# Products with v of two head pairs at once, FFN columns on both sides of the turning, and a later place for VectorE's first weight conversion of a slot

## The chip, the cores and the metric

The kernel runs on one core of a Trainium2 chip. The metric is the device time of one execution in microseconds (us); runs are compared by their medians. Beside the times there is a profile of one execution, which lists every instruction of the engines: PE (TensorE), DVE (VectorE), ACT (ScalarE), POOL (GpSimd), and SP, which here issues nearly all DMAs.

## The reference

Threshold attention, followed by a bilinear feed-forward layer (FFN). All data are float32: 8 batches, 8 heads, 576 positions, head width 64; the FFN has 4608 tokens, width 512, inner width 1536.

```python
scores = (q @ k.T) / sqrt(64)                       # per batch and head: 576 x 576
scores = where(scores >= max(scores) - tau, scores, -1e9)
attn = exp(scores - max(scores)); attn = attn / (sum(attn) + 1e-9)
x = (attn @ v)                                      # heads side by side: 4608 x 512
out = ((x @ w_a) * (x @ w_b)) @ w_out
```

## The kernel before

**Units and slots.** Two heads of a batch form a pair (batch b, hp 0 to 3; 32 pairs). The 576 query rows of a pair are cut into four units of 128 rows (u = 0 to 3), and the last 64 rows of two neighbouring pairs form one more unit (u = 4). The list `units` holds all 144 of them; for the first batch it starts with u = 0 of the pairs 0 to 3, then u = 1 of the pairs 0 to 3, so units 0 and 1 belong to pairs 0 and 1, units 2 and 3 to pairs 2 and 3, and so on. The main loop (from L1117, `for g in range(...)`) makes one slot per unit, and later stages of earlier units are done in the same slot. The instructions of an engine run in the order in which this loop emits them: `keep_order` fixes it. So an instruction that waits holds up all that stand behind it on its engine.

**One slot.** `scores` (L404) multiplies q and k of unit g on PE into two PSUM tiles, `sc`. DVE takes the maximum of each row (L411) and the threshold (L412). `weigh` (L422 to L438) makes exponentials on ACT (L431, L432) and multiplies them by the threshold's mask on DVE (L435), which also gives the row sums. These masks are the last readers of `sc`. A reciprocal of the sums on DVE (L448) and a scaling on ACT (L454) normalise the weights. Then the weights have to be turned, since the product with v contracts over the keys.

**Two ways to turn.** The first eight units (`BY_PE = 8`) are turned on PE in the next slot, `turn_pe` (from L472): 18 matmuls (each shows as two in the profile, as all float32 matmuls do) against a diagonal matrix that holds the reciprocals; ACT copies eight of the nine turned blocks from PSUM (L485), DVE the ninth (L486). All later units are turned by DVE transposes of 32x32 blocks (`turn_blocks`, L502) and two DMAs through a scratch tensor (`swap`), which SP issues.

**Products with v.** For a unit that PE turned, `weighted_unit` (L594) runs two slots after its scores: `product` (L538 to L547) makes 36 matmuls of 64x64 with 64 moving columns, ACT copies one half of the result to x (L553) and DVE the other (L554, two copies of 64x64), and POOL copies x to a second tile `xS` with the halves of the partitions exchanged (L569). For the later units, `weighted` and `weighted_tails` do the same with more columns; `weighted_tails` (L619) already treats two pairs in one product (L629).

**FFN columns.** As soon as x of a block is there, the generator `ffn` emits its matmuls in steps. `advance(cols)` takes as many steps as make up `cols` moving columns, so FFN work fills PE between the attention's parts. In slots 0 to 8 this is one call a slot, behind the turning (L1204); later slots have four calls with fixed portions. The first block is made in pieces of 128 columns: products `pab` with w_a (copied by ACT, L860) and w_b (multiplied by DVE, L862).

**Weights.** The weights w_a, w_b and w_out are read as 36 pieces of 128x512 values in 64 bits and are brought to float32 bit by bit on the chip: `convert_first` on ACT (L298, L299), `convert_clamp` on POOL (L305), `convert_sign` (L311) and `convert_shift` (L319) on DVE, `convert_add` on POOL (L324). Slots 0 to 3 begin two pieces each, slots 4 to 9 three, slots 10 to 14 two. A piece that is begun in one slot gets its last three steps in the next, by `convert_rest(g, k)`: k = 0 for the slot's first piece, ahead of the masks (L1147), k = 1 and k = 2 for the others, behind the masks (L1202, L1205).

**PSUM.** All PSUM tiles come from one pool of four buffers (`banks`), each two banks long. A new tile takes a buffer whose readers are done, so a matmul can wait for a mask, a copy or an `h` product on DVE.

Of the kernel before, what the change touches and what calls it, by code (L numbers as in the profile page):

```python
# [23 lines left out]
BY_PE = 8  # L24
# [30 lines left out]
def kernel(  # L55
# [38 lines left out]
    nc = tc.nc  # L94
    B, H, S, D = q.shape
    P = 128
# [3 lines left out]
    HP = H // 2  # L100
    NT = 4
    MAIN = NT * P
    TAIL = S - MAIN
# [8 lines left out]
    NSLOT = 9  # L112
# [15 lines left out]
    def banks(n, name):  # L128

        return psum.tile([P, 2, 512], FP32, tag="banks", name=name)[:, :, 0:n]  # L130
# [4 lines left out]
    loaded = {}  # L135
# [90 lines left out]
    for f in range(NG):  # L226
        for c in range(HP):
            for dst, w in ((wa_sb, w_a), (wb_sb, w_b)):
                src = []
                for r in range(2):  # L230
                    chunks = [(2 * c + e) % HP * 2 + (r + (c >= HP // 2)) % 2 for e in range(2)]
                    cols = slice(f * CW + r * CH, f * CW + (r + 1) * CH)
                    rows = w[:, cols].bitcast(U32).rearrange("(k p) f -> p k f", p=D)
                    src.append(rows[:, chunks[0]:chunks[1] + 1:2])
                pieces.append((dst[:, f, 2 * c:2 * c + 2].rearrange("p k f -> p (k f)"), src))
    for F in range(NF):
# [3 lines left out]
    state = {"loaded": 0, "added": 0, "converted": 0, "rows": 0, "sums": False, "through": 0, "over": False,  # L240
             "layer": False, "paced": False, "all": False, "turn": 0, "due": NPIECES, "wide": True, "slot": 0, "reading": False, "first": 0}
# [114 lines left out]
    x_of, xtail_of = {}, {}  # L356
# [4 lines left out]
    def prep(i, name):  # L361

        flush((name, i))
        mT = loaded[i].pop(name).rearrange("p n e -> p (n e)")
        nc.vector.transpose(mT, mT)
        prepared.setdefault(i, {})[name] = mT
# [105 lines left out]
    def turn_pe(i, u):  # L472

        ws, dg = weights.pop((i, u))
        ws = [w.rearrange("p n e -> p (n e)") for w in ws]
        wT = turned_tile()[:, 0:G].rearrange("p g s e -> p (g s e)").rearrange("p (s w) -> p s w", w=P)
        turned[i, u, "pe"] = [wT[:, :, y * D:(y + 1) * D] for y in range(2)]
        tp = banks(512, "tp").rearrange("p y (s q) -> p y s q", s=NT)
        last = banks(P, "tp")
        for s in range(NSLOT):  # L480
            for j, w in enumerate(ws):
                to = (last[:, 0] if s == 2 * NT else tp[:, s // NT, s % NT])[j * D:(j + 1) * D]
                nc.tensor.matmul(to, w[:, s * D:(s + 1) * D], dg[:, j], start=True, stop=True)
        for y in range(2):
            nc.scalar.copy(wT[:, y * NT:(y + 1) * NT], tp[:, y])  # L485
        nc.vector.tensor_copy(wT[:, 2 * NT], last[:, 0])  # L486
# [51 lines left out]
    def product(wT, vm, n):  # L538

        pv = banks(n // 2, "pv")  # L540
        for s in range(NSLOT):
            for j in range(2):
                rows = slice(j * D, (j + 1) * D)
                for c in range(2):
                    y = j ^ c
                    nc.tensor.matmul(pv[c * D:(c + 1) * D, y], vm[rows, s], wT[y](rows, s),  # L546
                                     start=(s == 0), stop=(s == NSLOT - 1))  # L547
        return pv

    def settle(out, pv, c0, c1, others):  # L550

        n = c1 - c0
        one = [nc.scalar.copy(out[:, 0:n], pv[:, 0, c0:c1])]  # L553
        two = [nc.vector.tensor_copy(out[c * D:(c + 1) * D, n:2 * n], pv[(1 - c) * D:(2 - c) * D, 1, c0:c1])  # L554
               for c in range(2)]
        for mine, theirs in ((one, others[1] + two), (two, others[0] + one)):
            for a in mine:
                for b in theirs:
                    tc.declare_no_dep(a.ins, b.ins, reason="banks of their own")
        others[0].extend(one)  # L560
        others[1].extend(two)
# [4 lines left out]
    def exchange(x, xs, hp, c0, c1, engine):  # L566

        for r in range(2):
            engine.tensor_copy(xs[r * D:(r + 1) * D, hp, c0:c1], x[(1 - r) * D:(2 - r) * D, hp, c0:c1])  # L569
# [21 lines left out]
                    exchange(x_of[key], xs, hp, 0, HALF, nc.gpsimd)  # L591
                ahead[key] = xs, count

    def weighted_unit(i, u):  # L594

        b, hp = pairs[i]
        wT = turned.pop((i, u, "pe"))
        pv = product([lambda rows, s, t=t: t[rows, s] for t in wT], loaded[i]["v"], P)
        settled_of[i] = settled_of.get(i, 0) + P
        if (b, 0) not in x_of:  # L600
            x_of[b, 0] = x_tile("xT")
            state["xs"] = x_tile("xS")
        settle(x_of[b, 0][:, hp, u * P:(u + 1) * P], pv, 0, D, ([], []))
        exchange(x_of[b, 0], state["xs"], hp, u * P, (u + 1) * P, nc.gpsimd)
        if hp == HP - 1:
            state["rows"] = u + 1
            if u == 0:
                blocks.append(((x_of[b, 0], state["xs"]), ("first", b, 0)))

    def tails(x, pv, hp, c0, c1):  # L610

        copies = [(nc.scalar.copy if j == c else nc.vector.tensor_copy)(
            x[j * D:(j + 1) * D, hp + c, c0:c1], pv[c * D:(c + 1) * D, j]) for c in range(2) for j in range(2)]
        for n, a in enumerate(copies):
            for m, b in enumerate(copies[:n]):
                if (n in (0, 3)) != (m in (0, 3)):
                    tc.declare_no_dep(a.ins, b.ins, reason="partitions of their own")

    def weighted_tails(i):  # L619

        b, hp = pairs[i]
        flush(("v", i), ("v", i + 1), ("wT", i, 2))
        t = turned.pop((i, NT))
        pv = banks(TAIL, "pv")
        for s in range(NSLOT):
            for j in range(2):
                rows = slice(j * D, (j + 1) * D)
                for c in range(2):
                    nc.tensor.matmul(pv[c * D:(c + 1) * D, j], loaded[i + c]["v"][rows, s],  # L629
                                     t[rows, 2 * c:2 * c + 2, s], start=(s == 0), stop=(s == NSLOT - 1))  # L630
        if hp == 0 and b % GT == 0:
            xtail_of[b // GT] = x_tile("xt")
        t = b % GT
        tails(xtail_of[b // GT], pv, hp, t * TAIL, (t + 1) * TAIL)
        for p in (i, i + 1):
            settled_of[p] = settled_of.get(p, 0) + TAIL
            if settled_of[p] == S:
                del loaded[p], prepared[p]
# [385 lines left out]
    def advance(cols):  # L1024
        running["owed"] += cols
        while running["owed"] > 0:
            if running["ffn"] is None:
                exchange_blocks()
                if not blocks:
                    running["owed"] = 0.0  # L1030
                    return
                if len(blocks[0][0]) == 4 and state["first"] == 3 * SEVENS:
                    for group in range(SEVENS):
                        first_sums(3, group)
                    state["first"] += 1
                if state["over"] and not state["all"]:
                    first_sums(3, SEVENS)
                    state["all"] = True
                running["tiles"] = len(blocks[0][0])
                running["ffn"] = ffn(*blocks.pop(0))  # L1040
                running["left"] = cost()
            step, rest, whole = next(running["ffn"], (None, 0, 0))
            if step == 0:
                running["owed"] = 0.0
                return
            if step is None:
                running["ffn"] = None
                state["through"] += 1
            else:
                running["owed"] -= step  # L1050
                running["left"] -= step
                passed(step)
                running["done"] = running["done"] + step if rest else 0
                running["rest"] = rest
                running["room"] = min(ROOM, whole // 2)
# [24 lines left out]
    units = []  # L1080
# [24 lines left out]
    def convert_rest(g, k):  # L1105

        for n in early.get(g - 1, [])[k:k + 1]:
            convert_sign(n)
            convert_shift(n)
            convert_add(n)  # L1110
# [6 lines left out]
    for g in range(len(units) + PV_LAG):  # L1117
# [22 lines left out]
            pace = min(pace, backlog() / (min([a for a in arrivals if a > g] + [len(units) + PV_LAG + 1]) - g))  # L1140
        pace += NSLOT * S / (2 * NT + 1) + CATCH_UP * max(backlog() - BLOCK_COLS, 0)
        if 2 <= g < BY_PE + 2:
            weighted_unit(*units[g - 2])
            running["owed"] -= NSLOT * P // 2
        if g < 3:
            prep_copy(*prep_pe(g + 1, "q"))
        convert_rest(g, 0)  # L1147
        if g == 0:
            for c in range(0, 2 * QUARTER - 2 * CW + 1, 2 * CW):
                extra.append(more_u32[:, c:c + 2 * CW].rearrange("p (f w) -> p f w", w=2))  # L1150
# [10 lines left out]
        for p in range(HP, NPR):  # L1161
            for name, d in (("q0", 1), ("q1", 1)):
                if g == (second if name == "q1" else first)[p] - d - (name == "q1" and p % 2):
                    prep(p, name)
        if here and g < BY_PE:
            reciprocal(i, u, nc.vector)
        if g < 3:
            kT, tp = prep_pe(g + 1, "k")
            nc.scalar.copy(kT.rearrange("p (c k) -> p c k", c=2), tp)
        if 0 < g <= BY_PE:  # L1170
            turn_pe(*units[g - 1])
        if g > BY_PE:
# [28 lines left out]
            normalise(i, u)  # L1201
        convert_rest(g, 1)  # L1202
        if g <= BY_PE:
            advance(pace)  # L1204
        convert_rest(g, 2)  # L1205
        for n in early.get(g, [])[1:]:
            convert_first(n)
# [74 lines left out]
```

## Time and profile before

| what | value |
|---|---|
| median of 3 runs | 1402.33 us (1402.2 to 1406.92) |
| profiled execution | 1400.57 us |
| its span, first to last instruction | 1398.8 us |
| mean granted clock of PE | 0.998 |
| 0 to 24 us: PE busy, DVE busy | 16.33, 11.75 us |
| 24 to 88 us (64 us long) | 52.78, 59.79 us |
| 88 to 165 us (77 us long) | 70.83, 74.53 us |
| 165 to 1398 us (1233 us long) | 1221.52, 867.85 us |

The profile's page gives, for the whole span, the busy time of each engine and its share; then the span in 40 equal slices of 35 us, one digit each (9 stands for 90% and more); then the DMA queues, the chain of work that ended last, and the costliest groups of instructions. A row of a timeline reads: start, length, engine, line of the kernel, operation, tiles written and read, shape, number of merged instructions, and in brackets the idle time just before it with what ended it. Weight conversions end at 140.85 us (the last L319), so all of the code that the change touches runs in the first 150 us or so.

### The profile page before, as it was taken

Reading aid. Unit: us, or ns where it says so; the run is one execution under the profiler, and the core shown is the slowest. Engines: PE = TensorE matmul, PEld = TensorE weight load, DVE = VectorE, ACT = ScalarE, POOL = GpSimd, SP = SyncE. Lnnn points to the kernel's source line nnn. Section 1 sums busy time; section 2 is a strip of 40 time slices with the busy share of each in tenths; the row PEclk is TensorE's granted clock in tenths of the full one; section 3 lists DMA queues with packets and bytes.
Section 4 is the critical chain, followed back from the end, with each engine's and each line's share of the span. In section 5 each row is a group of like instructions: output and inputs, shape, how many; then the busy total and the mean of one; then the engine's idle time right before and its main releaser. Section 6 shows DMA issues by size and latency. Waiting matters only on the chain.

```text
span 1398.8 us, 76307 instructions
## 1 busy us (share of the span) xinstructions
PE 1361.5 (97%) x33836; PEld 1258.5 (90%) x33836; DVE 1013.9 (72%) x2205; ACT 680.8 (49%) x1248; POOL 492.8 (35%) x675
## 2 busy tenths in 40 slices
PE   7889999999999999999999999999999999999998
PEld 5677588999998799999999999998899998799998
DVE  6999877787777768786767776778777776745425
ACT  6977555545554555544454545454545455431110
POOL 2764543424150607060515142332515060708100
PEclk9999999999999999999999999999999999999999
DMA  9977876667666775676556775566656775550000
GB/s 211 241 212 223 204 206 173 174 170 187 174 154 168 190 192 155 176 190 160 143 143 160 186 180 159 136 190 169 181 130 161 199 190 154 137 146 19 4 19 18
DMA packets 327449, 223.21 MB, mean 160 GB/s; under 512 B 171600, under 2 KB 311632, under 8 KB 327120
## 3 DMA queue, kind: packets, MB, share of 16 engines
q1 hardware_dynamic: 323936, 216.95, 60.1%
q8 instruction: 266, 4.36, 1.3%
q10 hardware_dynamic: 3184, 1.38, 0.4%
q14 instruction: 63, 0.52, 0.1%
HBM read 128.58 MB, written 89.65 MB: 156 GB/s over the span
## 4 chain that ended last, share of the span: by engine, by line
PE 88%; DMA 5%; DVE 4%; SPq 2%; issue 1%; ACT 1%; ACTq 0%; DVEq 0%
PE pab L750 29%; PE po L920 22%; PE pab L854 18%; PE sc L404 9%; PE pv L546 9%; SPq L144 1%; DMA vm<-in_v_dram 1%; DMA wT<-swap 1%; DVE tw L435 1%; DVE mx L411 1%; DMA more_u<-in_moe_w_a_dram 1%; DVE low L311 0%; DMA more_u<-in_moe_w_b_dram 0%; DVE tw L502 0%; DMA sums_u<-in_k_dram 0%
## 5 line engine op out<-in xcount | busy, mean ns | idle before, releaser
L454 ACT ACTIVATE tw<-tw,rcp 128x576 f32<-128x576 f32 x272 | 196.1, 768 | 201.3 <-DVE rcp L448 201.3
L411 DVE TENSOR_REDUCE mx<-sc 128x1 f32<-128x576 f32 x288 | 204.6, 752 | 121.2 <-PE sc L404 120.9
L432 ACT ACTIVATE tw<-sc,bias,scalars 128x576 f32<-128x576 f32 x288 | 239.6, 832 | 10.4 <-DMA qT<-in_q_dram 0.4
L712 POOL TENSOR_TENSOR h<-h,u 128x512 f32<-128x512 f32 x28 | 35.2, 1277 | 590.4 <-DVE h L824 414.1
L435 DVE SCALAR_TENSOR_TENSOR tw<-sc,thr,tw 128x576 f32<-128x576 f32 x288 | 220.9, 797 | 12.3 <-ACT tw L432 11.9
L920 PE MATMUL po<-wo_sb,h 64*64 64x256 f32 (+1 forms) x3408 | 210.5, 367 | 0.0
L502 DVE STREAM_TRANSPOSE tw<-tw 128x576 f32<-128x576 f32 x272 | 194.4, 752 | 0.8 <-ACT tw L454 0.8
L920 PEld LDWEIGHTS po<-wo_sb,h 64*64 64x64 f32 x3408 | 169.8, 133 | 14.9
L404 PE MATMUL sc<-kT,qT 64*64 64x288 f32 x2016 | 170.3, 404 | 1.8 <-issue 0.9
L546 PE MATMUL pv<-wT,vm 64*64 64x128 f32 (+2 forms) x4896 | 164.0, 275 | 3.7 <-DMA vm<-in_v_dram 1.4
L546 PEld LDWEIGHTS pv<-wT,vm 64*64 64x64 f32 x4896 | 153.2, 133 | 12.0 <-issue 4.0
L920 PE MATMUL po<-sums_u,h 64*64 64x256 f32 x2448 | 156.6, 376 | 0.0
L883 POOL TENSOR_TENSOR h<-h 128x256 f32<-128x256 f32 x168 | 117.2, 731 | 110.9 <-PE po L920 106.1
L750 PE MATMUL pab<-xU,wb_sb 64*64 64x128 f32 x4352 | 137.8, 269 | 0.0
L920 PEld LDWEIGHTS po<-sums_u,h 64*64 64x64 f32 x2448 | 126.1, 133 | 12.3 <-DVE h L862 0.5
L750 PEld LDWEIGHTS pab<-xU,wb_sb 64*64 64x64 f32 x4352 | 133.3, 133 | 1.8 <-ACT h L806 0.5
L404 PEld LDWEIGHTS sc<-kT,qT 64*64 64x64 f32 x2016 | 108.8, 133 | 17.3 <-issue 4.9
L431 ACT ACTIVATE bias<-mx,scalars 128x1 f32<-128x1 f32 x288 | 82.7, 287 | 66.1 <-DVE mx L411 65.6
L553 ACT COPY xT<-pv 128x128 f32<-128x128 f32 (+1 forms) x68 | 17.6, 259 | 193.5 <-PE pv L546 193.5
L750 PE MATMUL pab<-xS,wa_sb 64*64 64x128 f32 x2176 | 108.5, 269 | 0.8 <-issue 0.8
L554 DVE COPY xT<-pv 64x128 f32<-64x128 f32 (+1 forms) x136 | 38.1, 280 | 80.5 <-PE pv L546 79.0
L535 ACT COPY kept<-po 128x512 f32<-128x512 f32 x65 | 34.8, 535 | 120.3 <-PE po L920 106.4
(163 smaller groups left out, 2468.7 us busy)
## 6 DMA issues: line engine op xcount, KB each, us to landing
wT<-swap SPq DMA_DIRECT2D x242, 288.0 KB, 3.8
swap<-tw SPq DMA_DIRECT2D x480, 144.0 KB, 3.1
vm<-in_v_dram SPq DMA_DIRECT2D x128, 72.0 KB, 2.6
swap<-tw SPq DMA_DIRECT2D x128, 72.0 KB, 2.9
kT<-in_k_dram SPq DMA_DIRECT2D x112, 72.0 KB, 3.2
wT<-swap SPq DMA_DIRECT2D x56, 144.0 KB, 3.6
out_dram<-kept SPq DMA_DIRECT2D x27, 256.0 KB, 3.7
qT<-in_q_dram SPq DMA_DIRECT2D x112, 40.0 KB, 2.8
```

The lines of the kernel that those rows point to most:

```text
L404: nc.tensor.matmul(sc[m][o * D:o * D + wide, c], qT[r, q0:q0 + wide], kT[r, c * SH:(c + 1) * SH], start=True, stop=True)
L411: nc.vector.tensor_reduce(mx[:, c], sc[j], axis=AX.XY, op=ALU.max)
L431: nc.scalar.activation(bias[:, j:j + 1], mx[:, j:j + 1], AF.Copy, scale=e_nscale)
L432: nc.scalar.activation(wb[j], sb[j], AF.Exp, bias=bias[:, j:j + 1], scale=e_scale)
L435: nc.vector.scalar_tensor_tensor(out=wv, in0=sb[j], scalar=thr[:, j:j + 1], in1=wv, op0=ALU.is_ge, op1=ALU.mult, accum_out=sums[:, j:j + 1])
L454: nc.scalar.activation(w, w, AF.Copy, scale=rcp[:, j:j + 1])
L502: nc.vector.transpose(w, w)
L546: nc.tensor.matmul(pv[c * D:(c + 1) * D, y], vm[rows, s], wT[y](rows, s), start=(s == 0), stop=(s == NSLOT - 1))
L750: nc.tensor.matmul(out[c * D:(c + 1) * D, r, f * P:(f + 1) * P], w[g][k][rows, w0:w0 + D], moving[k][rows], start=(fresh and k == 0 and f ...
L854: nc.tensor.matmul(pab[c:c + columns(), r], w[rows, f // n, k, fs + c:fs + c + columns()], moving, start=(k == 0), stop=(k == H - 1))
L883: (nc.vector if state["over"] else nc.gpsimd).tensor_tensor(*a, **kw)
L920: nc.tensor.matmul(po[c * D:(c + 1) * D, r, y, cut], ht[rows, t0:t0 + D], other[rows, f, cut], start=(f == 0), stop=(f == NF // 2 - 1))
```

## The change

Three edits.

1. *Joint products.* The products of the eight units that PE turned are made for two pairs at a time, in the slots 3, 5, 7 and 9 (before: one unit in each of the slots 2 to 9). A new function `by_pairs` holds the loop that `weighted_tails` had: 36 matmuls whose moving side has all 128 columns of a unit; the two heads of pair i + c go to the partitions of half c. `tails` copies the result (two copies of 64x128 on ACT, two on DVE), and POOL exchanges both pairs in two copies.
2. *FFN columns.* In slots 0 to 8 the call `advance(pace)` behind the turning becomes `advance(pace / 2)` ahead of the turning and `advance(pace / 2)` at the old place.
3. *Conversion.* From slot 9 on `convert_rest(g, 0)` stands behind `weigh` (the masks) and the transposes of q for later pairs, and no longer ahead of the first FFN portion, the transposes of the weights (`turn_blocks`) and the masks.

```diff
-        turned[i, u, "pe"] = [wT[:, :, y * D:(y + 1) * D] for y in range(2)]
+        turned[i, u, "pe"] = wT
...
-    def weighted_unit(i, u):
+    def weighted_units(i, u):
 
         b, hp = pairs[i]
-        wT = turned.pop((i, u, "pe"))
-        pv = product([lambda rows, s, t=t: t[rows, s] for t in wT], loaded[i]["v"], P)
-        settled_of[i] = settled_of.get(i, 0) + P
+        wT = [turned.pop((i + c, u, "pe")) for c in range(2)]
+        pv = by_pairs(P, i, lambda rows, c, s: wT[c][rows, s])
...
-        settle(x_of[b, 0][:, hp, u * P:(u + 1) * P], pv, 0, D, ([], []))
-        exchange(x_of[b, 0], state["xs"], hp, u * P, (u + 1) * P, nc.gpsimd)
-        if hp == HP - 1:
+        x, xs, cols = x_of[b, 0], state["xs"], slice(u * P, (u + 1) * P)
+        tails(x, pv, hp, cols.start, cols.stop)
+        for r in range(2):
+            nc.gpsimd.tensor_copy(xs[r * D:(r + 1) * D, hp:hp + 2, cols], x[(1 - r) * D:(2 - r) * D, hp:hp + 2, cols])
+        for p in (i, i + 1):
+            settled_of[p] = settled_of.get(p, 0) + P
+        if hp + 1 == HP - 1:
...
+    def by_pairs(n, i, moving):
+
+        pv = banks(n, "pv")
+        for s in range(NSLOT):
+            for j in range(2):
+                rows = slice(j * D, (j + 1) * D)
+                for c in range(2):
+                    nc.tensor.matmul(pv[c * D:(c + 1) * D, j], loaded[i + c]["v"][rows, s], moving(rows, c, s),
+                                     start=(s == 0), stop=(s == NSLOT - 1))
+        return pv
...
         if 2 <= g < BY_PE + 2:
-            weighted_unit(*units[g - 2])
+            if g % 2:
+                weighted_units(*units[g - 3])
             running["owed"] -= NSLOT * P // 2
         if g < 3:
             prep_copy(*prep_pe(g + 1, "q"))
-        convert_rest(g, 0)
+        if g <= BY_PE:
+            convert_rest(g, 0)
...
+        if g > BY_PE:
+            convert_rest(g, 0)
         if here and g < BY_PE:
             reciprocal(i, u, nc.vector)
         if g < 3:
             kT, tp = prep_pe(g + 1, "k")
             nc.scalar.copy(kT.rearrange("p (c k) -> p c k", c=2), tp)
+        if g <= BY_PE:
+            advance(pace / 2)
         if 0 < g <= BY_PE:
             turn_pe(*units[g - 1])
...
         if g <= BY_PE:
-            advance(pace)
+            advance(pace / 2)
```

In the order of the changed program the instructions of every engine are the same as before, in the same sequence, from about the 18th slot to the end. Counted over the whole kernel, PE has 144 product matmuls of 128 columns in place of 288 of 64; DVE 8 copies of 64x128 in place of 16 of 64x64; ACT 8 copies of 64x128 in place of 8 of 128x64; POOL 8 copies of 64x2x128 in place of 16 of 64x128.

## The prediction

> **What bounds the kernel now.** I read the page's shares first, then the 40 slices, then the busy times of four stages of my choice, then the timelines of PE, DVE and POOL up to 165 us, and the waits of PE.
>
> ```profile
> PE 1361.5 (97%) x33836; PEld 1258.5 (90%) x33836; DVE 1013.9 (72%) x2205; ACT 680.8 (49%) x1248; POOL 492.8 (35%) x675
> PE   7889999999999999999999999999999999999998
> DVE  6999877787777768786767776778777776745425
> ```
>
> PE is the bound of the whole (97%), but in the first four slices (35 us each) it falls to 7 to 9 tenths, and there DVE stands at 9. The stages say it plainer (start:end, length, busy time of each engine, granted clock, DMA share, GB/s):
>
> ```profile
> 0.00:24.00 24.00, 16.33 (x94) 12.86 (x96) 11.75 (x32) 11.73 (x22) 3.20 (x9) 1.00 1.10 205
> 24.00:88.00 64.00, 52.78 (x1123) 45.78 (x1120) 59.79 (x132) 55.69 (x117) 47.10 (x57) 0.97 0.93 216
> 88.00:165.00 77.00, 70.83 (x1058) 55.25 (x1058) 74.53 (x159) 55.39 (x108) 44.26 (x42) 1.00 0.83 227
> 165.00:1398.00 1233.00, 1221.52 (x31576) 1144.59 (x31567) 867.85 (x1887) 557.95 (x1003) 398.18 (x568) 1.00 0.58 152
> ```
>
> From 24 to 88 us DVE (third figure) is busy 59.79 of 64 us and PE 52.78; from 88 to 165 us, 74.53 and 70.83 of 77. From 165 us on PE is 99% busy and has 11.5 us of idle time in all. So nothing can be won but in the first 165 us, where PE idles 25.1 us, 7.7 of them before 24 us. In the order of the changed program each engine's instructions are the same as before from about slot 18 (some 160 us) to the end; what counts is when DVE lets PE reach that point.
>
> A slot is one unit of scores; I count from 0, and its first DVE row is the maximum (L411): slot 3 begins at 31.68 us, 9 at 83.89, 16 at 141.29. These rows carry the sum:
>
> ```profile
> 24.34 1.28 PE L546 MATMUL pv<-wT,vm 64*64 64x64 f32 x72
> 32.87 1.26 PE L546 MATMUL pv<-wT,vm 64*64 64x64 f32 x68 [0.56 <-DMA vm<-in_v_dram]
> 78.36 2.08 PE L854 MATMUL pab<-xT,wa_sb 64*128 64x128 f32 x16 [1.45 <-DVE tw L435]
> 113.27 2.20 PE L546 MATMUL pv<-wT,vm 64*64 64x128 f32 x72
> ```
>
> ```profile
> 34.18 0.46 DVE L554 COPY xT<-pv 64x64 f32<-64x64 f32 x2 [0.66 <-PE pv L546]
> 80.97 1.49 DVE L319 TENSOR_SCALAR wb_sb<-wb_sb 128x512 uint32<-128x512 uint32 x1
> 83.89 1.42 DVE L411 TENSOR_REDUCE mx<-sc 128x1 f32<-128x576 f32 x2 [1.43 <-PE sc L404]
> 116.33 0.59 DVE L554 COPY xT<-pv 64x128 f32<-64x128 f32 x2
> ```
>
> ```profile
> 80.54 1.64 POOL L324 TENSOR_TENSOR wa_sb<-wa_sb,low 128x512 int32<-128x512 int32 x1 [0.96 <-DVE wa_sb L319]
> ```
>
> The reader is to see three things. A product of 64 columns takes 1.28 us, one of 128 columns 2.20. DVE has almost no idle time left: 0.66 us in slot 3, and 1.43 at 83.89, where PE was late because two groups of 16 matmuls took 2.08 and 1.81 us instead of 1.06 (the granted clock was 0.79 and 0.78 in the two 4 us stretches from 76 us). And an L319 that begins while POOL adds (L324) takes 1.49 us instead of 0.42: it ends with POOL's instruction, at 82.46 against 82.18.
>
> **The change, part by part.** *Joint products, PE.* Eight products of 64 columns (1.28) become four of 128 (2.20): 10.24 to 8.80, 1.4 us less. It is hidden: in slots 2 to 9 DVE sets the pace, and its cover gone it would be worth 1.4.
>
> *Joint products, DVE.* Eight pairs of copies of 64x64 (0.46 a pair) become four pairs of 64x128 (0.59): slots 2, 4, 6 and 8 lose 0.46, slots 3, 5, 7 and 9 gain 0.13. DVE is the bound here, so these count in full, except where a copy waits. ACT goes from one copy of 208 ns a slot to two of about 0.2 to 0.26 every second slot (128x64 and 128x128 rows as ends), POOL from 16 copies of 64x128 (509 ns) to 8 of twice the size: 8.1 us as before, by size; neither is in DVE's chain, and the first FFN group that reads the copies (xS) comes after a turning.
>
> *Slot 3.* This is the first new stall. Its product now needs v of pairs 0 and 1, and the second half of pair 1's v lands at 32.87 (the wait of 0.56 above). So the product of 2.20 ends at 35.05, where that of 64 columns ended at 34.13. DVE's copies stand ahead of the piece and the masks in the queue, and DVE waits longer than the 0.66 us. The 0.46 saved in slot 2 goes into this wait. Copies end at 35.65 against 34.64: +1.0. ACT's two copies and two exponentials then end about 37.8, 0.2 behind where the second mask would want them. I take **+1.2** at the end of slot 3 (bounds +0.6, if v lands earlier, and +1.5).
>
> *Slots 4 to 9.* Minus 3 x 0.46 plus 3 x 0.13: **-1.0**. In slots 5 and 7 the longer product still ends before DVE has finished maximum and threshold (copies start 1.2 and 0.9 us after the old product's end, and the new one takes 0.92 more); in slot 9 only 0.4 is left, so 0 to 0.9, I take **+0.4**.
>
> *FFN columns split around the turning.* Half of a slot's FFN matmuls (mostly one group of 16, 0.9 us) goes ahead of the turning (36 matmuls, 2.19). The last 4 matmuls of the turning take a bank that a mask frees, so they end about 0.5 us after the first mask, while DVE has the second mask and two small rows (1.2 us) before its copy of them: hidden. Where an h product ended between two L319, it lay under POOL's addition for nothing; in slots 6 and 8 it moves ahead of the turned tile's copy and costs its 0.33: 0 to 0.7, **+0.3**. For it, behind the second mask of slot 8 PE has one group and the scores less to do, so the 1.43 us of idle time before slot 9 can go: all of it at full clock, none if the clock falls again. I take half: **-0.7**.
>
> *Slots 9 to 15, the first piece behind the masks.* No row is removed; two rows (L311 and L319, about 1.0 us) go from before the transposes to behind the masks. Masks, transposes, and with them the swaps on SP's queue and PE's banks, come 1.0 us earlier in the slot: PE's waits of 1.07, 0.74 and 1.22 us at 89, 98 and 106 us are against that. The reciprocal and ACT's normalising (2 x 0.72) come 1.0 later; the next transposes are over 4 us behind, so this is covered. POOL's addition moves with the rows and stays in its place in POOL's queue, which is busy 44.26 of 77 us; the raw piece is freed 3 to 4 us later, but the loads stand ahead by a slot or more, and on SP's queue only two loads of w_out exchange their buffers: nothing for either. But DVE does the same work in a slot, and now two or three pieces stand in a row. Between one L319 and the next there were masks and more; now there is a reciprocal and L311 (0.7 us), with an h product 1.05, with the copies of a product 1.2 to 1.8. POOL's addition begins 0.1 us after an L319 ends (82.46 to 82.54) and takes 1.28, so it covers 1.38. What is short, DVE waits: slots 9 and 10, 0.33 each; 11, 0.68; 13, 0.18; 14, 0.08; 12 and 15 none: 1.6. Against that slot 10's L319 of 0.83 becomes 0.42, and the short waits for the reciprocal in slots 11 and 12 (0.27 and 0.18) vanish: 0.9 less. The lower end is no wait at all, -0.9, the upper end 7 x 1.08 (what the row of 1.49 has over 0.42) less the 0.9, 6.7. Five of the seven slots have something between the pieces, so the low end is nearer: I take 1.6 - 0.9, rounded, **+0.8**.
>
> The SBUF — State Buffer page of the Trainium skill (section "SBUF: two separate sides") states that VectorE in a 2-port mode and GpSimd share one pair of ports as an exclusive lock, held for a whole instruction. This trace agrees (1.49 against 0.42 us); by that rule alone, with every second piece meeting an addition, the term would be its upper end.
>
> *Slot 16.* DVE had waited 0.43 for PE at 141.29; a later DVE uses that: **-0.4**. At 145.33 PE waited 0.19 for the mask of slot 16, so beyond this DVE's lateness is PE's too.
>
> Sum: 1.2 - 1.0 + 0.4 + 0.3 - 0.7 + 0.8 - 0.4 = **+0.6 us**. The profiled execution took 1400.57 us (span 1398.8 and 1.8 around it), so it would take 1401.2; the median of the three runs is 1402.33, 1.8 above it, so the forecast is **1402.9**. Its own range, with the ends of the terms in part against each other, is 1400 to 1406.
>
> **The rivals.** *A: it gains.* If PE's waits on masks count more than DVE's queue, that is, if the additions of POOL fall beside h products and copies, the term of +0.8 becomes -0.9, the 1.43 us go whole (-0.7 more) and slot 3 costs 0.6 less: 0.6 - 1.7 - 0.7 - 0.6 = -2.4; with the 1.4 of PE's saved products at most -3.8. For it: PE's 5.9 us of waits on L435 in the first 200 us. Against it: DVE at 97%. Time 1398.5 to 1401, say **1400**.
>
> *B: PE's clock falls more often, and it is slower.* Slots 4, 6 and 8 lose their product, and their turning now ends before the masks: I count 1.7, 1.8 and 2.7 us of PE idle there. In the trace the clock fell where PE had worked 0.44 us in 2.9 us (75.5 to 78.4). If it falls in all three, each costs the 1.8 us of the two slow groups, and the idle time before slot 9 stays: 0.6 + 0.7 + 2 x 1.8 = +4.9, time **1407.2**. It decides from less than about half a us of PE work in 3 us. Against it: waits of 2.25 us at 58 us did not do it. The page TensorE: Matmul & The Clock Gate of the Trainium skill ("What's actually happening") puts the window at about 3.4 us; the trace agrees as far as one fall can show.
>
> *C: the lock holds in every slot.* Then +6.7 in place of +0.8, +6.5 in all: **1408.8**. For it: the three L319 of 1.49 to 1.51 us in slots 8 to 10, and two before. Against it: five of seven slots have an h product or copies between.
>
> *D: the change does not do what it says.* Its order has four joint products, the split and the late pieces, so only their effect can be nil: 1402.3, inside the forecast.
>
> **How the numbers follow.** Forecast with D 0.52, A 0.30, B 0.12, C 0.06. I call 0.5% (7.0 us, 1395.3 to 1409.3) about what a measurement of this kernel can tell from no change; all cases end inside it. From A's and from B's and C's far ends I give 0.04 and 0.05 to beyond. The range takes A and the near part of B: 1398 to 1407.5.
>
> **What would show it.** PE's product in slot 3 ending near 35.0 and DVE's copies waiting some 1.5 to 2 us for it (step slot 3); copies of 0.59 every second slot; no wait at the maximum of slot 9 and full clock near 78 us (else B); second L319 of slots 9, 10, 11 and 13 at 0.6 to 1.1 us (lock term); slot 16 beginning 0.5 to 1.5 us later than 141.29. Wrong would be a DVE busy time to 165 us that falls by more than 2 us, or a PE that idles more after 165 us than 11.5 us.

## The result, and the profile after

The changed kernel takes **1414.03 us** (median of 6 runs, 1409.46 to 1417.2) beside 1402.26 us for the kernel before (6 runs, 1400.98 to 1406.92): ratio **1.0073**, 95% interval 1.0051 to 1.0095. The forecast was 1402.9 and its range ended at 1407.5, so the time lies outside, on the slow side. The profiled execution took 1414.56 us (span 1412.8, mean granted clock 0.995), 14.0 more than that of before.

The busy times and two of the rows of slices, from the page of the changed kernel:

```profile
PE 1365.5 (97%) x33548; PEld 1257.2 (89%) x33548; DVE 1016.7 (72%) x2197; ACT 681.5 (48%) x1248; POOL 492.7 (35%) x667
PE   6888999999999999999999999999999999999998
DVE  5899886788777777776757776777777776745424
```

PE was meant to have 1.4 us less work and has 4.0 more; DVE 2.8 more. The four stages of before, in the changed kernel (start:end, length, busy time of PE, PEld, DVE, ACT and POOL, granted clock, DMA share, GB/s):

```profile
0.00:24.00 24.00, 13.31 (x102) 10.21 (x102) 13.43 (x35) 14.11 (x28) 5.61 (x12) 1.00 1.11 204
24.00:88.00 64.00, 51.89 (x779) 45.06 (x778) 54.14 (x114) 51.54 (x104) 40.18 (x43) 0.89 0.90 211
88.00:165.00 77.00, 68.87 (x976) 54.19 (x972) 75.78 (x148) 54.37 (x106) 46.42 (x45) 1.00 0.80 209
165.00:1398.00 1233.00, 1222.09 (x31487) 1140.55 (x31484) 868.14 (x1890) 560.28 (x1009) 399.79 (x569) 1.00 0.58 153
```

Two things have changed. From 24 to 88 us the granted clock is 0.89 (before 0.97): PE is busy nearly as long as before and gets less far, and DVE is idle for 9.9 of 64 us where it was idle for 4.2. From 88 to 165 us the clock is full, and there DVE is busy 75.78 of 77 us, 1.3 more than before. So there are two losses, in two stages, of two kinds. The start of each slot (the first maximum, L411, of a slot) dates them. Against the profile of before, slot 9 begins 2.6 us later, slot 15 9.0, slot 16 8.3, slot 20 8.3, slot 140 13.3. What comes after slot 20 can't be put down to the change: from slot 20 to slot 140 the first profile of before takes 1037.5 us, the shortest of all profiles here, a second profile of before (below) 1043.5 and the changed kernel 1042.5.

The rows that answer to those of the prediction, PE first (the lines of the code are 8 further down from L854 on; the product is L620, its copies L626):

```profile
33.72 2.20 PE L620 MATMUL pv<-wT,vm 64*64 64x128 f32 x72
62.86 0.44 PE L483 MATMUL tp<-first_u,tw 128*64 128x128 f32 x4 [2.66 <-DVE tw L435]
63.59 2.00 PE L862 MATMUL pab<-xT,wa_sb 64*128 64x128 f32 x16 [0.30 <-DVE tw L435]
```

The last two rows lie in slot 6, which has lost its product. PE waits 2.66 us for a mask, works 0.44 us, and the next group of 16 matmuls takes 2.00 us in place of about 1.06. That is the picture that the trace of before showed once, at 78 us. In the changed kernel the granted clock falls to half at 26.2, 46.7 and 63.7 us, each time behind waits of PE (2.90 us for a load, 1.67 and 2.66 for masks).

DVE and POOL in slot 10:

```profile
103.82 1.57 DVE L311 SCALAR_TENSOR_TENSOR more_u<-raw,more_u 128x512 uint32<-128x512 uint32 x1
105.31 0.83 DVE L319 TENSOR_SCALAR wo_sb<-wo_sb 128x512 uint32<-128x512 uint32 x1
106.06 0.68 DVE L311 SCALAR_TENSOR_TENSOR low<-more_u,low 128x512 uint32<-128x512 uint32 x1
106.66 1.49 DVE L319 TENSOR_SCALAR wo_sb<-wo_sb 128x512 uint32<-128x512 uint32 x1
```

```profile
103.57 1.27 POOL L324 TENSOR_TENSOR wb_sb<-wb_sb,low 128x512 int32<-128x512 int32 x1 [3.25 <-DVE wb_sb L319]
```

POOL's addition of the first piece runs from 103.57 to 104.84. The L311 of the second piece begins at 103.82, inside it, and takes 1.57 us in place of 0.68: it ends at 105.39, 0.55 after the addition. My sum had counted L311 as 0.7 us of cover for L319. It is no cover, it waits itself.

### The profile page after: what moved, and what is told of

It is laid out like the page before. It is cut to its first block, busy times and chain, and to the rows that moved or that the text cites. A ratio compares the mean times of both kernels' runs of the same rounds, so it can differ in the third digit from the quotient of the medians.

```text
span 1412.8 us, 75716 instructions
## 1 busy us (share of the span) xinstructions
PE 1365.5 (97%) x33548; PEld 1257.2 (89%) x33548; DVE 1016.7 (72%) x2197; ACT 681.5 (48%) x1248; POOL 492.7 (35%) x667
## 4 chain that ended last, share of the span: by engine, by line
PE 86%; DVE 6%; DMA 3%; SPq 2%; issue 1%; ACT 1%; ACTq 0%; DVEq 0%
PE pab L758 30%; PE po L928 22%; PE pab L862 17%; PE sc L404 9%; PE pv L546 9%; SPq L144 1%; DMA wT<-swap 1%; DVE mx L411 1%; DVE low L311 1%; DVE tw L435 1%; DMA sums_u<-in_k_dram 1%; DVE tw L502 1%; SPq L198 1%; DMA kT<-in_k_dram 0%; DVE wo_sb L319 0%
## 5 line engine op out<-in xcount | busy, mean ns | idle before, releaser
L411 DVE TENSOR_REDUCE mx<-sc 128x1 f32<-128x576 f32 x288 | 204.4, 751 | 120.6 <-PE sc L404 120.2
L435 DVE SCALAR_TENSOR_TENSOR tw<-sc,thr,tw 128x576 f32<-128x576 f32 x288 | 221.0, 797 | 12.7 <-ACT tw L432 12.4
L928 PE MATMUL po<-wo_sb,h 64*64 64x256 f32 (+1 forms) x3408 | 215.6, 367 | 0.0
L502 DVE STREAM_TRANSPOSE tw<-tw 128x576 f32<-128x576 f32 x272 | 194.3, 752 | 0.8 <-ACT tw L454 0.8
L404 PE MATMUL sc<-kT,qT 64*64 64x288 f32 x2016 | 176.6, 404 | 1.7 <-DVE xt L554 1.2
L928 PE MATMUL po<-sums_u,h 64*64 64x256 f32 x2448 | 159.5, 376 | 0.0
L546 PE MATMUL pv<-wT,vm 64*64 64x128 f32 (+1 forms) x4320 | 155.5, 282 | 3.3 <-DMA wT<-swap 1.8
L546 PEld LDWEIGHTS pv<-wT,vm 64*64 64x64 f32 x4320 | 145.1, 133 | 8.2 <-issue 3.3
L404 PEld LDWEIGHTS sc<-kT,qT 64*64 64x64 f32 x2016 | 111.7, 133 | 17.8 <-issue 3.8
L758 PE MATMUL pab<-xS,wa_sb 64*64 64x128 f32 x2176 | 112.6, 269 | 1.5 <-issue 1.5
L553 ACT COPY xT<-pv 128x128 f32<-128x128 f32 x60 | 15.9, 265 | 193.2 <-PE pv L546 193.2
L758 PEld LDWEIGHTS pab<-xS,wa_sb 64*64 64x64 f32 x2176 | 94.0, 133 | 2.2 <-issue 2.0
L758 PE MATMUL pab<-xT,wa_sb 64*64 64x128 f32 x1856 | 95.9, 269 | 0.0
```

Of the source, the lines that this page charges most:

```text
L404: nc.tensor.matmul(sc[m][o * D:o * D + wide, c], qT[r, q0:q0 + wide], kT[r, c * SH:(c + 1) * SH], start=True, stop=True)
L411: nc.vector.tensor_reduce(mx[:, c], sc[j], axis=AX.XY, op=ALU.max)
L435: nc.vector.scalar_tensor_tensor(out=wv, in0=sb[j], scalar=thr[:, j:j + 1], in1=wv, op0=ALU.is_ge, op1=ALU.mult, accum_out=sums[:, j:j + 1])
L502: nc.vector.transpose(w, w)
L758: nc.tensor.matmul(out[c * D:(c + 1) * D, r, f * P:(f + 1) * P], w[g][k][rows, w0:w0 + D], moving[k][rows], start=(fresh and k == 0 and f ...
L928: nc.tensor.matmul(po[c * D:(c + 1) * D, r, y, cut], ht[rows, t0:t0 + D], other[rows, f, cut], start=(f == 0), stop=(f == NF // 2 - 1))
```

## The experiments

Each kernel is dated by the starts of its slots against the first profile of before. The two intervals that matter are "to slot 9" (edits 1 and 2) and "slot 9 to 16" (edit 3). The experiments ran on several chips; times and ratios are against the kernel before on the same chip.

### One edit at a time

**late_only** is before with edit 3 alone, **joint_only** before with edit 1, **split_only** before with edit 2, **no_late** the changed kernel without edit 3. Edit 3 in short:

```diff
-        convert_rest(g, 0)
+        if g <= BY_PE:
+            convert_rest(g, 0)
...
             weigh(i, u)
+        if g > BY_PE:
+            convert_rest(g, 0)
```

> The kernel before with the third edit alone (from slot 9 on the first piece's L311 and L319 stand behind the masks). Theory Lock: the pieces of a slot now follow each other, DVE meets POOL's additions, and DVE loses 0.6 to 1.3 us a slot in slots 9 to 15, as in the changed kernel (its slot 15 was 8.96 us late, slot 9 only 2.62): slot 9 begins as before (within 0.5 us of 83.89 us), slot 16 begins 5 to 6.5 us later than 141.29; the time is 4 to 7 us above the kernel before. Rival Start: the lateness of slots 9 to 15 is what the late start of the first slots drags along (loads, swaps, PE out of step): then with the third edit alone slot 16 is within 1.5 us of before, and the time within 2 us.

> The kernel before with the joint products alone (first edit). Theory Slot 2: with no product in slot 2 PE stands idle while the q and k rows of pair 3 land (1.99 and 2.90 us in the changed kernel), the granted clock halves, the turning takes 4.1 us in place of 2.2, and slot 3 begins 1.5 to 2.5 us later than 31.68; from there to slot 9 nothing more is lost. The time is 1 to 4 us above before. Rival Split: the loss up to slot 9 comes from the FFN columns ahead of the turning; then slot 3 is late here too, but slots 5 to 8 are not later than slot 3 by more than 0.5, and the product's saved 1.4 us and copies' 1.0 show as slot 9 beginning no later than before.

> The kernel before with the second edit alone (half of the FFN columns ahead of the turning in slots 0 to 8). Theory: worth nothing by itself, 1 us either way, since DVE sets the pace and every FFN group is still made in its slot; slot 16 begins within 1.5 us of 141.29. Rival Split: the turning waits longer for masks (2.66 and 3.65 us in slots 6 and 8 of the changed kernel), PE's clock falls, and slots 6 to 8 get 1 to 2 us later.

> The changed kernel without its third edit (the first piece's conversion stays ahead of the masks in all slots). Theory Lock: the 6.3 us lost between slots 9 and 15 are gone, slot 16 begins 1.5 to 3.5 us later than 141.29, and the time is 1405 us, 2 to 5 above before. Rival Start: they stay, slot 16 begins over 6 us late, time above 1409.

Measured on one chip (before there 1408.84, 32 runs); the clock is the mean granted clock over all timed runs, 0.9956 for before:

| kernel | median | ratio, interval | clock | slot 9 late by | slot 9 to 16 longer by |
|---|---|---|---|---|---|
| late_only | 1410.91 | 1.0032, 1.0010 to 1.0054 | 0.9957 | -2.3 | +5.5 |
| joint_only | 1413.95 | 1.0042, 1.0018 to 1.0065 | 0.9932 | +7.9 | +0.6 |
| split_only | 1411.08 | 1.0023, 1.0008 to 1.0038 | 0.9958 | +2.0 | +0.3 |
| no_late | 1415.05 | 1.0045, 1.0026 to 1.0064 | 0.9934 | +3.7 | +0.4 |

So each loss has its edit. The stretch from slot 9 to 16 grows by 5.5 us with edit 3 and by at most 0.6 without it. The low clock comes with edit 1 and without edit 3. What the starts of slots alone can't tell is whether the low clock is a cause, and that is tried further down. Edit 2 alone costs a little too; its clock is that of before.

The column on slot 9 has to be read with care. Up to there late_only, the two late kernels of the next part and before run the same code, and in their five profiles slot 9 begins between 81.6 and 85.1 us. So only joint_only and no_late stand clearly outside this spread. Several expectations missed: late_only began slot 9 2.3 us early where 0.5 was the bound, joint_only lost far more by slot 9 than the fall in slot 2 alone would give, no_late was 6.3 us slower by its ratio where 2 to 5 were expected, and split_only had slot 16 2.3 us late where 1.5 was the bound.

### Is it POOL's additions?

**late_no_add** is late_only, and from slot 9 on POOL's additions are left out, with the shift turned the other way so that the weights stay finite; it doesn't compute the reference. **late_adds_last** is late_only with the additions of a slot written behind its last L319. **before_again** is the kernel before, once more, with a profile.

```diff
 # late_no_add
-            convert_add(n)
+            if g <= BY_PE:
+                convert_add(n)
+            elif n in stages:
+                stages.pop(n)
+                state["added"] += 1
 # late_adds_last
-            convert_add(n)
+            if g <= BY_PE:
+                convert_add(n)
+        if g > BY_PE and k == 2:
+            for n in early.get(g - 1, []):
+                convert_add(n)
```

> The kernel before with the third edit, and from slot 9 on POOL's addition (L324) is left out; the shift of these pieces goes the other way, so that the weights stay finite (w_a, w_b and w_out are not the reference's from piece 20 on). DVE runs the same rows as with the third edit alone. Theory Lock: with no addition to meet, the 6.2 us that slots 9 to 15 lost with the third edit alone are gone, and so is the 1.08 us that before itself loses in slots 9 and 10: slot 16 begins 1 to 3 us earlier, counted from slot 9, than before. Rival Order: the loss comes of the order itself (h products and reciprocals later, PE waiting for them), and 3 to 6 us stay.

> The kernel before with the third edit, and from slot 9 on all of POOL's additions of a slot are emitted behind the slot's last L319, nothing left out. Theory Lock: L311 and L319 of one slot meet no addition; the additions now lie beside the next slot's maxima, where the threshold (L412) may wait for one: 1 to 3 of the 6.2 us stay. Rival Order: 5 to 6 us stay.

> The kernel before once more, for its slots on this chip, since single executions spread over 10 us. All theories: slots 3 to 20 begin within 2 us of those of the first profile (31.68, 83.89, 141.29, 167.60 us), with a fall of PE's granted clock, if any, in slot 8. Where the changed kernels are later by more than this control's own difference, it is the change.

Measured (one execution each, beside before at 1406.0, 13 runs): late_no_add 1403.63 us, slot 9 to 16 **2.3 us shorter** than before; late_adds_last 1406.53, 4.2 longer (4.9 to slot 15, 3.0 to slot 17); before_again 1407.98, 0.4 longer. Without the additions edit 3 makes the stretch shorter. The price with them shows in DVE's groups between slots 9 and 16 (busy, mean ns), first before, then the changed kernel with filled slots (**after_fill**, below), which has the same 16 L311 and 16 L319 there:

```profile
L319 DVE TENSOR_SCALAR wo_sb<-wo_sb 128x512 uint32<-128x512 uint32 x12 | 6.1, 507 | 0.0
L311 DVE SCALAR_TENSOR_TENSOR low<-sums_u,low 128x512 uint32<-128x512 uint32 x5 | 3.4, 683 | 0.0
...
L311 DVE SCALAR_TENSOR_TENSOR low<-more_u,low 128x512 uint32<-128x512 uint32 x3 | 2.0, 679 | 0.0
```

```profile
L319 DVE TENSOR_SCALAR wo_sb<-wo_sb 128x512 uint32<-128x512 uint32 x12 | 8.8, 734 | 0.0
L311 DVE SCALAR_TENSOR_TENSOR low<-sums_u,low 128x512 uint32<-128x512 uint32 x5 | 5.1, 1027 | 0.0
...
L311 DVE SCALAR_TENSOR_TENSOR low<-more_u,low 128x512 uint32<-128x512 uint32 x3 | 2.7, 888 | 0.0
```

All of L311 together goes from 10.9 to 14.3 us and all of L319 from 9.4 to 11.9: +3.4 and +2.5, together 5.9. The stretch itself is 5.9 us longer (63.31 against 57.40). The account closes to half a microsecond: DVE's other rows take 0.5 more there and its idle time is 0.5 less. In late_no_add L319 (L321 in that kernel) has 433 ns in the same group. Where did the additions go before? Beside the transposes (L502) and masks (L435) that followed the first piece: the one of 96.82 to 98.10 us there lies under a pair of transposes of 1.42 us and a mask of 0.77, their usual times.

late_adds_last missed, and the trace says why:

```profile
98.32 0.41 DVE L319 TENSOR_SCALAR wb_sb<-wb_sb 128x512 uint32<-128x512 uint32 x1
98.99 0.15 DVE L448 RECIPROCAL rcp<-sums 128x2 f32<-128x2 f32 x1
99.07 1.58 DVE L311 SCALAR_TENSOR_TENSOR more_u<-raw,more_u 128x512 uint32<-128x512 uint32 x1
```

```profile
98.82 1.27 POOL L324 TENSOR_TENSOR wb_sb<-wb_sb,low 128x512 int32<-128x512 int32 x1 [1.26 <-DVE wb_sb L319]
```

Its addition of the first piece still begins 0.09 us after that piece's L319 (98.73), and the next L311 still takes 1.58. Where POOL is free, an addition waits for its own operands only; that it is written behind DVE's later rows doesn't hold it back. The edit moved the additions behind POOL's other rows of the slot, no more. So the edit does not test the lock theory ("the lock", as in the prediction, is POOL's addition holding up the DVE row beside it); that the lock takes L311 as well, it shows again.

before_again gave a warning of another kind. Slot 2 begins 2.9 us earlier than in the first profile, slot 3 2.0 later; between them PE waited 2.90 us for k rows, and its turning then ran at half the clock:

```profile
26.73 1.19 PE L378 MATMUL tp<-more_u,sums_u 96*128 96x96 f32 x6 [2.90 <-DMA sums_u<-in_k_dram]
27.86 4.11 PE L483 MATMUL tp<-first_u,tw 128*64 128x128 f32 x36
```

The changed kernel's profile has the same two rows (2.90 and 4.11), and I had taken them for the change's alone. The change is not needed for them: the clock falls in slot 2 in one of the six profiles of kernels without edit 1, and in four of the five that have edit 1 and no fill (below). After them before_again is on time again at slot 9 (-0.4), and slot 16 (-0.1), and late at slot 140 (+6.1).

### Is the clock a cause?

The joint products leave slots 2, 4, 6 and 8 without a product. **joint_fill** is joint_only with a product of 64 columns in these slots that nobody reads; **split_fill** and **after_fill** put the same into no_late and into the whole change. They add work and compute the reference as well. **after_again** is the changed kernel, **joint_again** joint_only, each with a second profile.

```diff
             if g % 2:
                 weighted_units(*units[g - 3])
+            else:
+                i0, u0 = units[g - 2]
+                by_half(i0, turned[i0, u0, "pe"])
...
+    def by_half(i, wT):
+
+        pv = banks(D, "pv")
+        for s in range(NSLOT):
+            for j in range(2):
+                rows = slice(j * D, (j + 1) * D)
+                for c in range(2):
+                    y = j ^ c
+                    nc.tensor.matmul(pv[c * D:(c + 1) * D, y], loaded[i]["v"][rows, s],
+                                     wT[rows, s, y * D:(y + 1) * D],
+                                     start=(s == 0), stop=(s == NSLOT - 1))
```

> The kernel before with the joint products, and in slots 2, 4, 6 and 8 a product of 64 columns whose result nobody reads (the matmuls that stood there before: 1.28 us each, 5.1 us of PE work more). Theory Clock: PE is not silent in these slots, the granted clock stays at 1.0 through 40 to 92 us, and slot 9 begins 3 to 7 us earlier than with the joint products alone (91.81); the time is 2 to 5 us below it although PE does more work. In slot 2 the k rows of pair 3 still land near 27 us, so slot 3 is late by 0.5 to 1. Rival Copies: the loss comes of the copies and exchanges that now wait for a longer product; then slot 9 begins at 91 us or later.

> Edits 1 and 2 together (joint products, split ffn columns; edit 3 left out), with unread products of 64 columns on TensorE in slots 2, 4, 6 and 8, the slots that the joint products leave without one. It tells whether the loss of edits 1 and 2 (ratio 1.0045 in no_late) hangs on the clock. Clock theory: the fill adds some 5 us of TensorE's work and yet the kernel gains; mean granted clock of the runs 0.996 to 0.998 (joint_fill 0.998, no_late 0.993), ratio 1.000 to 1.004. Theory of waits (the joint products cost by what TensorE waits for, and the clock only follows): the fill's work comes on top, ratio 1.006 to 1.009, clock 0.993 to 0.995.

> The whole change with the same unread products in slots 2, 4, 6 and 8. Clock theory and lock theory together: the clock's part goes and the lock's part of slots 9 to 16 stays, so slot 9 begins within 2 us of where it does without edit 1, slot 16 begins 4 to 6 us later against slot 9 than before, ratio 1.002 to 1.006, clock 0.996 to 0.998. If the clock is not a cause: ratio 1.008 to 1.012, clock 0.992 to 0.995. If the lock's part was only a chance of one execution: slot 16 against slot 9 within 1.5 us of before.

> The changed kernel once more, on the chip of the filled ones, with a second profile. If the loss is the kernel's: ratio 1.004 to 1.010, clock of the runs 0.992 to 0.995, and slot 16 begins 4 to 7 us later against slot 9 than before, as in the first profile (5.6). If much of it was the chip's: ratio under 1.003.

> Edit 1 alone, a second profile. Clock theory: granted clock under 0.8 in at least four of the fifteen windows of 4 us from 24 to 84, and slot 9 begins 3 to 9 us later than before (7.9 in the first profile). Theory of chance: at most two such windows, as in the profiles of before, and slot 9 within 2 us of before.

Measured, joint_fill on the chip of the three runs above (before 1406.0), the others on one chip (before 1407.0, 23 runs); the clock of before was 0.9963 on both:

| kernel | median | ratio, interval | clock | slot 9 late by | slot 9 to 16 longer by |
|---|---|---|---|---|---|
| joint_fill | 1409.22 | 1.0015, 0.9998 to 1.0033 | 0.9979 | +0.9 | +0.5 |
| split_fill | 1406.92 | **1.0001**, 0.9977 to 1.0024 | 0.9975 | -2.5 | +0.5 |
| after_fill | 1412.21 | **1.0040**, 1.0017 to 1.0063 | 0.9970 | +0.8 | +5.9 |
| after_again | 1418.56 | **1.0079**, 1.0051 to 1.0108 | 0.9941 | -0.5 | +5.7 |
| joint_again | 1416.48 (one run) | | 0.993 | +4.0 | +0.6 |

About 5 us of useless work (4 x 1.28) make the changed kernel 6.4 us *faster* (1418.56 to 1412.21; 4.9 by the means of the runs). Edits 1 and 2 with the fill take what before takes. What is left of after_fill's loss, 1412.21 against split_fill's 1406.92, is 5.3 us, the lock's. So of the loss of 11.6 us on this chip about 6 go with the fill and 5.3 with the lock. That the fill's part is the clock's fits in size: a mean clock of 0.9941 in place of 0.9970 over some 1412 us is 4.1 us of full clock lost. No run sets the clock by itself, so waits that the fill shortens may have a share. Slot 6 of joint_only, then the same place in split_fill:

```profile
59.01 1.97 PE L483 MATMUL tp<-first_u,tw 128*64 128x128 f32 x32
64.13 0.70 PE L483 MATMUL tp<-first_u,tw 128*64 128x128 f32 x4 [3.15 <-DVE tw L435]
64.76 2.08 PE L862 MATMUL pab<-xS,wb_sb 64*128 64x128 f32 x16
66.63 1.92 PE L862 MATMUL pab<-xT,wa_sb 64*128 64x128 f32 x16
```

```profile
56.32 1.97 PE L483 MATMUL tp<-first_u,tw 128*64 128x128 f32 x32
58.59 0.44 PE L483 MATMUL tp<-first_u,tw 128*64 128x128 f32 x4 [0.31 <-DVE tw L435]
59.34 1.16 PE L874 MATMUL pab<-xT,wa_sb 64*128 64x128 f32 x16 [0.30 <-DVE tw L435]
```

With the product, and by edit 2 an FFN group, ahead of it the turning comes later in the slot, PE waits 0.31 us for the mask instead of 3.15, and the group behind it (L874 is the L862 of the other kernels) runs at full clock. Edit 2 without the fill does not do this: no_late has the FFN group there and its clock falls at 64.7 us. From 24 to 88 us the granted clock is 0.81 in joint_only, 0.89 in joint_again, no_late and the first profile of after, 0.97 in after_again and after_fill, 0.95 in joint_fill and 1.00 in split_fill. joint_again had three stretches of 4 us under 0.8 where at least four were expected and slot 9 4.0 us late, inside what the clock theory gave. joint_fill was to keep full clock from 40 to 92 us and fell once there, at 62.1. Time at half clock between 24 and 92 us is 3.4 to 10.2 us in the six profiles without edit 1, 3.4 to 27.3 in the five with it and no fill (four of them at 13.7 or more), and 0 to 6.8 in the three with the fill. The number of falls differs from one execution to the next, and it is the mean of the timed runs that is steady: 0.993 to 0.994 for joint_only, no_late and both sets of after, 0.997 to 0.998 for the three filled kernels, 0.996 for before.

## Why the prediction was wrong, by its own steps

**The step that failed first is the term of slots 9 to 15**, "the first piece behind the masks": +0.8 in the sum. Slot 15 begins 6.2 to 6.6 us later against slot 9 in late_only, both profiles of after and after_fill. The mechanism was named, and the upper end (6.7) was near in size, but in part by luck: it counted L319 alone, which gained 2.5. What I chose within the bounds was wrong, for a reason that I gave: "Five of the seven slots have something between the pieces". What stands between them is mostly an L311, and I had it down as 0.7 us of cover. The 3.4 us that L311 gained were in no term. The trace of before had the row that says so, an L311 of 1.66 us at 71.88 beside 0.68 elsewhere. The SBUF — State Buffer page of the Trainium skill (section "SBUF: two separate sides") states that a VectorE operation with two SBUF inputs takes the shared ports too, against a GpSimd operation that reads SBUF. I had quoted the other half of that sentence. The runs agree: 0.68 to 1.57 us for L311, which reads two tiles. Rival C, which held that the lock acts in every slot, was right in size, with the same luck, and had 0.06.

**The second is the term before slot 9**, half of 1.43 us gained, with rival B at 0.12. B had its mechanism right (the even slots have no product, the turning ends early, PE idles, the clock falls) and its places in part: it named slots 4, 6 and 8, and the first profile of after falls in slots 2, 4 and 6. So the sign I gave for B, a fall near 78 us and a wait at the maximum of slot 9, looked in the wrong place: that profile has neither. Its evidence against, that 2.25 us of waiting near 58 us did not bring a fall, was one execution's luck: the wait lay across two of the stretches of 3.41 us by which the clock changes (see the last section), with PE busy 1.76 us in the one and 2.82 in the other. A row's history in a single trace doesn't bound what another execution, with those stretches at other places, will do. B's price was 4.9 in all, with nothing of C; the two came together.

Of the other steps:
- *Slot 3* held roughly: +1.2 expected, slot 3 takes 2.0 us longer in after_again, 2.2 in after_fill; the unchanged code takes 7.0 to 8.4 us there, 7.5 in the first profile. The product ends at 34.95 in after_again (expected 35.0), and the copies wait 1.83 us (expected 1.5 to 2). In the first profile of after the slot itself was 2.1 late and the wait only 0.48.
- *Slots 4 to 9*, with the split: -1.0 in the sum (-1.0, +0.4, +0.3, -0.7). after_again gains 1.8 from slot 4 to 9, after_fill 1.4, split_fill 2.7, against the 44.7 us of the first profile of before. But the same code takes 42.7 us in before_again, late_only and late_adds_last, where no fall lies just ahead of slot 9, and 45.5 in late_no_add. Only split_fill, with no fall there at all, is shorter than all of these, by 0.7. So gains of this size can hardly be told from the spread of executions, and this part of the sum is neither shown nor refuted.
- *Slot 16* held: -0.4 expected, -0.7 in late_only, in both profiles of after and in after_fill.
- *What would show it wrong*: DVE's busy time to 165 us fell by 2.7 us (146.07 to 143.35), which was on the list; PE's idle time after 165 us is 10.9 us, below the bound of 11.5. Of the 14.0 us between the two profiles 8.3 are there at slot 20.

**What stays open**: why split_only, with the clock of before, is 1.0023 (1.0008 to 1.0038); with the joint products and the fill this is gone. Its one profile has two falls of the clock from 24 to 88 us, before's first has one, but over all timed runs the clocks agree (0.9958 and 0.9956). And no run put the additions where nothing collides with them, so the 2.3 us that late_no_add gains in slots 9 to 16 were not had with a kernel that computes the reference. None of the kernels that do was faster than before.

## What to carry to other kernels

Before work is moved on one engine, look at what the next engine does with its result at once: here DVE's conversion releases an addition on POOL, and the old place was good because transposes and masks, which the addition doesn't hold up, stood behind it. When rows of an operation show two durations (0.68 and 1.66, 0.42 and 1.49), price every neighbour of the moved row by the longer one, and take both for bounds only if the trace says which applies. Work taken from an engine with short idle times can cost more than it saves: four products fewer in the wrong slots cost some 6 us, most of it clock, and a useless product in them gave it back.

## What the runs showed of the hardware

- The clock changes in steps of 3.41 us. In all fourteen profiles every fall before 200 us lasts 3.41 or 6.83 us at half clock, and the falls of one execution begin whole multiples of 3.41 us apart: 26.17, 46.65 and 63.72 us in the first profile of after (6 and 5 steps), 60.52 alone in after_again. The Trainium skill's page TensorE: Matmul & The Clock Gate (section "What's actually happening") gives a window of about 3.4 us that runs freely, and half the clock after an idle one; the traces agree on the window.
- The window need not be idle. Cut from 20 to 95 us into these steps, the fourteen profiles have 12 steps with PE busy under 1.3 us, and all 12 are followed by half clock; of the 54 with 1.3 to 2.3 us 16 are, and of the 242 with more only 5, each inside a fall that had begun. So it matters where a wait lies. In the first profile of after the wait of 2.66 us in slot 6 lies in one step (PE busy 0.56 us) and the clock falls; the longer one of 3.65 us in slot 8 is split between two (1.46 and 1.72) and it doesn't. The steps lie at other places in each execution, which fits with one kernel falling three times in one execution and once in the next. The bounds of 1.3 and 2.3 us are read from these profiles alone.
- The lock works both ways: POOL's clamp (L305), 0.62 us in late_no_add's mean, has 0.78 in late_only's, and a row behind an addition in slot 10 of after takes 1.05.
- An instruction on POOL that is written later need not run later: in late_adds_last most additions behind a wait on DVE began 0.08 to 0.09 us after their operands.
